# One evacuation per 16-row score, in a box of two PSUM banks, with all queues found anew

## Chip, cores and metric

The kernel runs on one core of a Trainium2 chip. The metric is device time in microseconds (us) of one execution, less is better. Engines are named as in the profile: PE (TensorE), DVE (VectorE), ACT (ScalarE), POOL (GpSimd), SP (SyncE, which issues the transfers).

## What is computed

A small neural codec: a depthwise filter of three taps over time, SiLU, four rounds of residual vector quantisation with codebooks of eight entries, and a second depthwise filter over the sum of the chosen entries.

```python
B, T, D, K = 2, 16000, 512, 3;  Nq, C = 4, 8          # all bf16
z = silu(sum(xp[:, i:i+T, :] * dw_enc[i] for i in range(K)))
res = z; q = 0
for s in range(Nq):
    cb = codebooks[s]
    d2 = |res|^2 - 2 res.cb^T + |cb|^2                # bf16 arithmetic, [B, T, C]
    sel = cb[d2.argmin(-1)]
    q = q + sel; res = res - sel
y = sum(qp[:, i:i+T, :] * dw_dec[i] for i in range(K))
```

## The kernel before, in words

**Tiles.** The 32,000 rows of time are cut into 18 tiles. A tile holds G rows of time on each of 128 partitions: G is 16 in fourteen of them, and 6 and 8 in the first and the last two. `split` (in the tile list) cuts a tile's G rows into stretches of SPLIT = 8 rows, so a 16-row tile has two.

**Stages of a tile.** Transposing loads bring x with its channels on the partitions (four groups of 128 channels). `front` works on one half (two channel groups) at a time: three taps as products with a weight per partition (lines 638 on ACT or 639 on DVE, into TA and TB), two additions of 4096 numbers (line 390, TA and ZB), the exponential on ACT (644), plus one (646 on DVE or 645 on ACT). `front2` does the reciprocal on ACT (656) and the product ZB <- ZB, EX (line 390), called the gate below. `select` scores the rows against the first three codebooks and decides one after the other (one-hot vectors OHA, OHD). `resid` subtracts the chosen entries from ZB on PE (833, 838) and casts the result back (860 on ACT or 861 on DVE), in four units of one channel group, each with a first and a second part, then scores the residual against the fourth codebook. `back` multiplies one-hot windows with the decoder's rows (910, 912, 914), casts the 1024 numbers to bf16 (919 on ACT or 920 on DVE, into YB) and stores them.

**A score.** `products` and `gram` let PE write 64 numbers for each row: 32 whose maximum is the row's squared norm (a mask product at line 668 sets the others very low), and the products with the 32 codebook entries (line 675). 8 rows fill one PSUM bank of 512 fp32. For each stretch of 8 rows `select` (key `score0`) evacuates with a reduce of 8 x 32 (line 709) and an addition of 8 x 24 (line 710), and `resid` (key `score3`) with a reduce of 8 x 32 (876) and a cast of 8 x 8 (877). All four run on DVE, and the bank comes free after them. Before the change a 16-row tile has two such boxes for each of its two scores.

**PSUM.** There are eight banks, as four pairs. `take=("S", box)` takes one bank, `take=("A", box)` an aligned pair. `resid` and `back` take pairs; `products` takes a pair when its stretch has more than 8 rows (`"SA"[g1 - g0 > NMK]`). At most four boxes may wait for DVE at a time.

**Order.** Nothing is scheduled at run time. Each step is put into a `Plan` with its engine, its readers and writers and a cost. Two long strings set the rest: RANK gives each step its place in its engine's queue, and WHERE says for each step that ACT or DVE could do (taps, plus one, casts out of PSUM) which of them does it. `Plan.order` walks the queues with the costs, hands out banks, and where it sees PE waiting for over a microsecond it puts fill matmuls in front of the next step (function `fill`, line 968: a product of 512 columns that nobody reads). Each engine then runs its queue in order and waits on semaphores.

Of the kernel before, what the change touches and what calls it, by code (L numbers as in the profile page):

```python
# [185 lines left out]
def kernel(  # L186
# [14 lines left out]
    KT = D // P  # L201
# [18 lines left out]
    RANK = ("0001020001010b0b0f0Z0g0W0i0Y0n04090n0o1c1q0n0x0q0y0h0l0r070R060k0D060A000s0j0l040E0e0C080f070v0a0g020c0e0h0i0j0l0o04050d"  # L220
            "0k0m0r0s0t02070g01030403080d0005060409060b050a0a0c0k0m0j0h0f090G0I0L0M0N0P0Q0l0q0s080t050J0j0o121718141e1s0q0f0i10151b0g"
            "080e090c0h0d030n0w0x0y070K0T0U0X0m0u0p0M0i0z03010t0B0a0m0o0H0r021f0v1k0b0u0F0p0e0V0k1a0c0O0d0S11130p16191d0w1g0A1p1i1j1h"
            "0z1l1n1m1o0B1v0C1y0D1A0r0s1I1J1K1M1N1O1P0p0t0J0u1R1T1U1W1X1Y1Z2021220q0v230w25262728292a2b2c0u0x0N0y0z2e0P0A0B2i2h0E0F0V"
            "0S0G0H0U0T0K0L2y2A2C2H2K0M2P0O120R130V0X351u1t1r1u1w1x0E1z1B0F0H1F1D1E1C1G0G1H1L0I0K0L2f0O2g0C0D2j2k2l2m2n2o2p0v0I2s0J2r"
            "2w2B2E2v2x2G2I2J2L0w0N0Z0P2N2Q2T2S2V2W2X2Y0x0Q110S0T15140U0V16190W0Y18370Z101b1a11123d3e3f3g3i131f1c1r171t1x1a1i161n1t03"
            "07020g080h0k060b0c0e0d0j09000f0a05241Q1S1V2d0R0Q2q0X2M2t2u2z0W2D0Y2F2R103317391c3h14153n18193t3u3v3x3z3B3D0y1b1l1d3G3I3L"
            "3M3K3N3O3P3Q3R0z1e1p1f3U3W3Y3X3Z4041420A1i441k1l1w1u1m1o1x1y1p1q1z1C1r1s1B4l1v1w4u1x1z4F4H4L4S4V1O1S20201W211V1V1V1X1Y1S"
            "1R1W23231Z212225242c0w0p0t0q0i0v0n0o0s0B0y0A0l0x0r0z0u0m2U302Z31323634381e1g3c1d3a3b3j3l3m3o1h3A1k3J1m3S1g1h431j1n494b4c"
            "4e4g4h4j0B1t4o1u4n4r4v4w4q4s4y4z4A4C0C1y4E1A4G4I4K4J4M4O4P4Q0D1C1G1E1F1J1I1H1J1N1M1K1L1P1O1M1N1Q1R1T1U5p1S1Z5z5E5H5J5M26"
            "5R2a272c292828262b28272r2l2x2r2n2s2m2t2p2t0T0N0F0D0S0K0E0R0M0P0Q0H0G0C0J0O0I0L3s3p3q3r3w1j3y3C1q451o3E3H3F3T1s3V461A4p1D"  # L230
            "4D1E4N1B1G4X1D1I4Z51525455572O580E1P1T1Q595b5e5g5l5n5o5q5t5v0G1Y5x225y5B5G5I5L5N5Q5S0I295W2e2g2c2b2h2i2e2d2k2m2k2g2n2o2j"
# [458 lines left out]
    def select(st):  # L690
        n, G = st["n"], st["G"]
        GC = G * C
        b = n % 2
# [119 lines left out]
    def resid(st):  # L813
        n, G = st["n"], st["G"]
        Z, W = zrows(st), OHR[n % 2]
# [48 lines left out]
        b = n % 2  # L864
# [141 lines left out]
```

## Time and profile before

| | us |
|---|---|
| median of three runs | 607.04 (604.66 to 607.81) |
| profiled execution, its time | 603.48 |
| its span, first to last instruction | 601.7 |
| PE busy, of it fill matmuls (L968) | 526.0, 131.9 |
| DVE busy | 567.5 |
| ACT busy | 547.5 |
| POOL busy | 60.7 |

Busy is the time in which at least one instruction of the engine was recorded. A matmul's record is longer than the time for which it holds up the next one, and the same holds for DVE and ACT instructions by a tenth of a microsecond. A group's row gives line, engine, operation, output <- inputs, shapes and count, then busy time and mean nanoseconds of one, then the engine's idle time just before the group and what ended it. A row of the timeline gives start and length in us. The granted TensorE clock was 0.994 over the span.

### The profile page before, as it was taken

The page shows a single profiled execution, that of the slowest core. Times are in us where ns is not written, and L with a number is a line of the kernel's source. Part 1 is how long each engine was busy: PE and PEld are TensorE (multiplying, and loading weights), DVE is VectorE, ACT ScalarE, POOL GpSimd, SP SyncE. Part 2 cuts the span into 40 slices and gives each one's busy share as a digit, 9 for nine tenths or more (in the row PEclk, how much of TensorE's full clock was granted, in tenths as well). Part 3 has the DMA queues.
Part 4 walks back from the last instruction along what each step waited for, and adds up shares of the span by engine and source line. Part 5 has one row for each costly group of instructions (what it writes and reads, how often), then busy time and mean ns, then how long its engine had stood idle before and what let it go on. Part 6 is the DMA issues. An engine that isn't in the chain of part 4 may idle for free.

```text
span 601.7 us, 28081 instructions
## 1 busy us (share of the span) xinstructions
PE 526.0 (87%) x12774; PEld 250.9 (42%) x12774; DVE 567.5 (94%) x1130; ACT 547.5 (91%) x423; POOL 60.7 (10%) x93
## 2 busy tenths in 40 slices
PE   5968889898888898899899888989988889989995
PEld 3424444334344344343444443443444344444552
DVE  6999999999999999999999989999999999999774
ACT  4898899999999999999999999999999999997554
POOL 3003100203101100000010011000001210110000
PEclk9999999999999999999999999999999999999998
DMA  9416356435556766565665668565494472204345
GB/s 216 94 44 91 65 93 111 104 66 82 146 94 140 130 165 116 148 139 89 169 108 98 154 112 175 108 144 140 89 198 125 108 142 82 107 5 142 109 141 189
DMA packets 155566, 71.87 MB, mean 119 GB/s; under 512 B 146895, under 2 KB 146927, under 8 KB 155318
## 3 DMA queue, kind: packets, MB, share of 16 engines
q1 hardware_dynamic: 155230, 69.64, 52.6%
q8 instruction: 100, 1.64, 1.1%
q10 hardware_dynamic: 216, 0.43, 0.4%
q14 instruction: 20, 0.16, 0.1%
HBM read 2.26 MB, written 32.77 MB: 58 GB/s over the span
## 4 chain that ended last, share of the span: by engine, by line
DVE 39%; ACT 19%; PE 17%; SPq 10%; issue 9%; DMA 4%; DVEq 0%; ACTq 0%
DVE ZB L390 8%; SPq L597 7%; DVE TB L639 6%; DVE TA L390 5%; PE banks L833 5%; ACT YB L919 5%; ACT EX L644 4%; DVE TA L639 4%; PE banks L838 3%; PE banks L910 3%; ACT EX L656 3%; PE banks L675 3%; ACT TB L638 2%; DVE EX L646 2%; ACT ZB L860 2%
## 5 line engine op out<-in xcount | busy, mean ns | idle before, releaser
L968 PE MATMUL banks<-MSK,IDENT 128*128 128x512 bf16 x555 | 131.9, 380 | 4.8 <-issue 2.3
L860 ACT CAST ZB<-banks 128x1024 bf16<-128x1024 f32 (+2 forms) x116 | 102.3, 938 | 20.1 <-PE banks L838 20.0
L644 ACT ACTIVATE EX<-ZB 128x4096 bf16<-128x4096 bf16 (+2 forms) x36 | 115.2, 3202 | 4.9 <-DVE ZB L390 4.7
L919 ACT CAST YB<-banks 128x1024 bf16<-128x1024 f32 x113 | 109.4, 1037 | 8.4 <-PE banks L910 7.1
L656 ACT ACTIVATE EX<-EX 128x4096 bf16<-128x4096 bf16 (+2 forms) x36 | 114.7, 3196 | 0.2
L675 PE MATMUL banks<-ZB 128*32 128x64 bf16 x8064 | 88.5, 196 | 5.1 <-DVE ZB L390 2.5
L675 PEld LDWEIGHTS <-ZB 128*32 128x32 bf16 x8064 | 75.4, 94 | 39.5 <-issue 33.6
L639 DVE TENSOR_SCALAR TB<-XT,WENC 128x2048 bf16<-128x2048 bf16 (+2 forms) x123 | 83.4, 689 | 0.8 <-DMA out_dram<-YB 0.5
L910 PE MATMUL banks<-WDEC,OHW 128*128 128x512 bf16 x252 | 73.2, 381 | 11.6 <-ACT ZB L860 3.2
L838 PE MATMUL banks<-OHR,WR 32*128 32x512 bf16 (+2 forms) x1152 | 82.0, 355 | 0.0
L747 POOL COPY OHD<-OHA 128x256 bf16<-128x256 bf16 (+2 forms) x36 | 39.6, 1099 | 401.6 <-DVE OHA L390 388.1
L968 PEld LDWEIGHTS <-IDENT 128*128 128x128 bf16 x555 | 50.6, 98 | 62.1 <-issue 8.0
L390 DVE TENSOR_TENSOR ZB<-TA,TB 128x4096 bf16<-128x4096 bf16 (+2 forms) x36 | 72.8, 2023 | 0.6 <-ACT TB L638 0.3
L390 DVE TENSOR_TENSOR TA<-TA,TB 128x4096 bf16<-128x4096 bf16 (+2 forms) x36 | 73.2, 2032 | 0.1
L390 DVE TENSOR_TENSOR ZB<-ZB,EX 128x4096 bf16<-128x4096 bf16 (+2 forms) x36 | 72.7, 2022 | 0.1
L833 PE MATMUL banks<-ZB,IDENT 64*64 64x512 bf16 (+2 forms) x576 | 55.5, 367 | 10.5 <-ACT ZB L860 3.8
L833 PE MATMUL banks<-ZB,UP 64*64 64x512 bf16 (+2 forms) x576 | 52.7, 351 | 0.0
L639 DVE TENSOR_SCALAR TA<-XT,WENC 128x2048 bf16<-128x2048 bf16 (+2 forms) x67 | 45.1, 681 | 3.0 <-DMA XT<-in_x_dram 2.0
L838 PEld LDWEIGHTS <-WR 32*128 32x128 bf16 x1152 | 23.3, 92 | 58.6 <-issue 50.4
L833 PE MATMUL banks<-ZB,DOWN 64*64 64x512 bf16 (+2 forms) x576 | 41.5, 363 | 0.0
L638 ACT ACTIVATE TB<-XT,WENC 128x2048 bf16<-128x2048 bf16 (+2 forms) x21 | 35.0, 1672 | 2.4 <-DVE TA L390 1.8
L646 DVE TENSOR_SCALAR EX<-EX 128x4096 bf16<-128x4096 bf16 (+2 forms) x33 | 36.8, 1115 | 0.0
(133 smaller groups left out, 591.3 us busy)
## 6 DMA issues: line engine op xcount, KB each, us to landing
out_dram<-YB SPq DMA_DIRECT2D x33, 448.0 KB
out_dram<-YB SPq DMA_DIRECT2D x28, 512.0 KB
XT<-in_x_dram SPq DMA_TRANSPOSE x267
out_dram<-YB SPq DMA_DIRECT2D x30, 60.0 KB
ZB<-in_x_dram SPq DMA_DIRECT2D x1, 1024.0 KB
ZB<-in_x_dram SPq DMA_DIRECT2D x1, 768.0 KB
out_dram<-YB SPq DMA_DIRECT2D x31, 2.0 KB
out_dram<-YB SPq DMA_DIRECT2D x2, 224.0 KB
```

Of the source, the lines that this page charges most:

```text
L390: add("DVE", cost, key, lambda: nc.vector.tensor_tensor(out=out, in0=a, in1=b, op=op), reads, writes, **kw)
L639: lambda dst=dst, src=src, w=w: nc.vector.tensor_scalar(out=dst, in0=src, scalar1=w, scalar2=None, op0=ALU.mult),
L644: add("ACT", act(2 * R), ("exp", n, h), lambda: nc.scalar.activation(v(ex), Z, ACT.Exp, scale=-1.0), zt, [("EX", sl), "ACTTAB"], hold="E")
L646: lambda: nc.vector.tensor_scalar(out=ex, in0=ex, scalar1=1.0, scalar2=None, op0=ALU.add), [], [("EX", sl)])
L656: nc.scalar.add_instruction(mybir.InstActivation(name=nc.get_next_instruction_name(), engine=mybir.EngineType.Activation, func=ACT.Reciprocal,
L675: nc.tensor.matmul(o[HB * q:HB * (q + 1), u * ZW:(u + 1) * ZW].rearrange("p (s c) -> p s c", s=2), lhsT=blk, rhs=both, start=False, stop=( ...
L833: nc.tensor.matmul(at(r)[to], lhsT=dia[h, h], rhs=Z[h, i, r:G:RG, :], start=start, stop=False)
L838: nc.tensor.matmul(at(r), lhsT=WR[v][g, i * P:(i + 1) * P], rhs=W[g, v // 3, 0:rows_of[r], :], start=False, stop=stop)
L860: either({"ACT": act_psum(2 * k * P), "DVE": dve(2 * k * P)}, key(1), lambda dst=dst, src=src: nc.scalar.copy(dst, src()), lambda dst=dst, ...
L910: nc.tensor.matmul(o, lhsT=W[:, k, PADC:PADC + P], rhs=WDEC[u], start=True, stop=not wrap)
L919: either({"ACT": act_psum(1024), "DVE": dve(1024)}, key, lambda dst=dst, box=box: nc.scalar.copy(dst, ps(box)), lambda dst=dst, box=box: n ...
L968: nc.tensor.matmul(PS[j // 2][:, 512 * (j % 2):512 * (j % 2) + NMK * ZW], lhsT=IDENT, rhs=MSK.rearrange("p u w -> p (u w)"), start=True, s ...
```

## The change

Both scores take all G rows of a tile as one stretch. For a 16-row tile the box is then a pair of banks; the two mask products, the 16 groups of row products and their order inside a score remain, and one reduce of 16 x 32 with one addition of 16 x 24 (or one cast of 16 x 8) follows the last of them. The first row products now wait for the ZB tokens of both stretches, which the gate and the casts write anyway. Tiles of 6 and 8 rows have one stretch as before.

With other steps in the plan, RANK and WHERE are replaced by new strings. They differ nearly everywhere, so the order of every queue and the engine of some taps, casts and additions are other ones, and so are the number and places of the fill matmuls, which follow from the order.

```diff
-    RANK = ("0001020001010b0b0f0Z0g0W0i0Y0n04090n0o1c1q0n0x0q0y0h0l0r070R060k0D060A000s0j0l040E0e0C080f070v0a0g020c0e0h0i0j0l0o04050d"
...
+    RANK = ("00010200010c0b0b0h0j0i0X0f0l0m02020j0q0w0A0n0v0p0x0j0p0u080H07030D0q0v040k0e0r020x0N0T090n070s0r0d0406090a0f0k0o0q010e0g"
...
-    WHERE = ("ADDDADDAAAADADDDDADDADDDDADDDADADADDAAAADAADDDDDADADDDDADADAAAAAAAADAAAAAAADDDDAADDDDAADDAADAAAAAAADAAAAAAAAADDDDDDADADDDD"
...
+    WHERE = ("AADAAAAAAAADDDDDDDDDDDDDDDDDADAAAADDAADAAADDDDDADADDDDADADAAAAAAADAAADAAADDDDADDDDDAADDADDAAAADADAADAAAAAADDDDDDDDDDDAD"
...
@@ select
-        zt = lambda q: [("Z", st["zb"], i, st["zq"] + q, b) for i in range(KT) for b in range(2)] + [("ZC", st["zb"])]
+        zt = lambda q: [("Z", st["zb"], i, st["zq"] + k, b) for k in range(len(st["split"])) for i in range(KT) for b in range(2)] + [("ZC", st["zb"])]
         nq = len(st["split"])
-        for q, (g0, g1) in enumerate(st["split"]):
+        for q, (g0, g1) in enumerate([(0, G)]):
@@ resid
-        zt = lambda q: [("Z", st["zb"], i, st["zq"] + q, b) for i in range(KT) for b in range(2)] + [("ZC", st["zb"])]
+        zt = lambda q: [("Z", st["zb"], i, st["zq"] + k, b) for k in range(len(st["split"])) for i in range(KT) for b in range(2)] + [("ZC", st["zb"])]
         nq = len(st["split"])
-        for q, (g0, g1) in enumerate(st["split"]):
+        for q, (g0, g1) in enumerate([(0, G)]):
```

91 lines of the change are left out of this document (45 added, 46 removed).

## Prediction, made before the changed kernel ran

> **What bounds the kernel now.** I read the page's busy lines first, then its slices, then busy time by window, then groups by form, and last the timeline around a score and at the end.
>
> ```profile
> span 601.7 us, 28081 instructions
> PE 526.0 (87%) x12774; PEld 250.9 (42%) x12774; DVE 567.5 (94%) x1130; ACT 547.5 (91%) x423; POOL 60.7 (10%) x93
> ...
> DVE  6999999999999999999999989999999999999774
> ACT  4898899999999999999999999999999999997554
> ```
> ```profile
> 0.00:60.00 60.00, 45.80 (x607) 23.95 (x611) 52.32 (x156) 44.59 (x60) 9.91 (x37) 1.00 0.56 111
> 60.00:540.00 480.00, 426.44 (x10656) 200.51 (x10656) 471.59 (x857) 468.48 (x325) 48.41 (x49) 1.00 0.56 118
> 540.00:555.00 15.00, 13.93 (x406) 6.24 (x403) 13.56 (x39) 11.31 (x11) 1.43 (x3) 1.00 0.41 143
> 555.00:592.00 37.00, 37.00 (x1105) 19.08 (x1103) 28.55 (x80) 20.12 (x27) 0.94 (x4) 1.00 0.38 131
> 592.00:602.00 10.00, 2.83 (x13) 1.09 (x12) 1.45 (x3) 3.03 (x4) 0.00 (x0) 0.82 0.57 177
> ```
> In a window row the columns are length, then busy time of PE, PEld, DVE, ACT and POOL. There are two regimes. From 60 to 540 us DVE is busy 471.59 of 480 us and ACT 468.48: DVE is idle for 8.4 us in all, ACT for 11.5. From 555 to 592 us PE is busy without a gap while DVE has 8 us and ACT 17 us to spare. The border is the last gate, the product that finishes the encoder output of the last tile:
>
> ```profile
> 548.05 0.41 PE L833 MATMUL banks<-ZB,IDENT 64*64 64x512 bf16 x4
> ...
> 550.25 0.41 PE L833 MATMUL banks<-ZB,IDENT 64*64 64x512 bf16 x4
> ...
> 552.91 0.95 DVE L390 TENSOR_TENSOR ZB<-ZB,EX 128x1536 bf16<-128x1536 bf16 x1
> ...
> 554.96 0.34 PE L668 MATMUL banks<-MSK,IDENT 128*128 128x384 bf16 x1
> ...
> 593.28 2.91 ACT L919 CAST YB<-banks 128x1024 bf16<-128x1024 f32 x3 [1.16 <-PE banks L910]
> ```
> It ends at 553.86; PE starts the last tile's first score at 554.96, and 46.7 us later the span ends. So I forecast in two pieces: how much DVE and ACT must do up to the last gate, and how much PE has behind it.
>
> **What one instruction costs its engine.** Recorded lengths overlap, so I take start to start:
>
> ```profile
> 304.91 0.42 DVE L876 TENSOR_REDUCE rr<-banks 128x8 bf16<-128x256 f32 x1
> 305.25 0.21 DVE L877 CAST PR<-banks 128x64 bf16<-128x64 f32 x1
> 305.38 0.28 DVE L725 TENSOR_TENSOR RC<-banks,S 128x128 f32<-128x128 f32 x1
> 305.58 0.28 DVE L390 TENSOR_TENSOR V<-PR,rr 128x128 bf16<-128x128 bf16 x1
> ...
> 537.78 3.80 ACT L919 CAST YB<-banks 128x1024 bf16<-128x1024 f32 x4
> 538.35 0.29 DVE L736 TENSOR_REDUCE M<-KEY 128x16 f32<-128x128 f32 x1
> 538.67 0.29 DVE L390 TENSOR_TENSOR OHA<-KEY,M 128x128 bf16<-128x128 f32 x1
> ...
> 540.00 0.35 DVE L710 TENSOR_TENSOR S<-banks,CC 128x192 f32<-128x192 f32 x1
> 540.26 0.17 DVE L390 TENSOR_TENSOR TR<-rr,RD 128x16 bf16<-128x16 f32 x1
> ```
> A reduce of 256 numbers holds DVE for 0.34 us, a cast of 64 for 0.13, an addition of 192 for 0.26, one of 128 for 0.20, each 0.08 less than its recorded length. From 64 to 256 numbers that is 0.21 us for 192, so about 1.05 ns a number over a fixed 0.065 us. An instruction that needs the one just before it starts 0.32 us after it (538.35 to 538.67) and not 0.20: 0.12 lost. On ACT four casts of 1.04 take 3.80, so 0.92 each.
>
> **The change, part by part.** (1) Evacuations. A 16-row score has one pair of DVE instructions over 16 rows instead of two pairs over 8:
>
> ```profile
> L709 DVE TENSOR_REDUCE rr<-banks 128x8 f32<-128x256 f32 x30 | 12.5, 417 | 0.6 <-PE banks L675 0.6
> L710 DVE TENSOR_TENSOR S<-banks,CC 128x192 f32<-128x192 f32 x30 | 10.4, 347 | 0.0
> L876 DVE TENSOR_REDUCE rr<-banks 128x8 bf16<-128x256 f32 x30 | 12.5, 417 | 1.8 <-PE banks L675 1.8
> L877 DVE CAST PR<-banks 128x64 bf16<-128x64 f32 x30 | 6.4, 213 | 0.0
> ...
> L920 DVE CAST YB<-banks 128x1024 bf16<-128x1024 f32 x13 | 15.9, 1219 | 4.7 <-PE banks L910 2.6 <-ACT ZB L860 1.0 <-PE banks L914 1.0
> L919 ACT CAST YB<-banks 128x1024 bf16<-128x1024 f32 x113 | 109.4, 1037 | 8.4 <-PE banks L910 7.1 <-ACT EX L644 0.7 <-DMA out_dram<-YB 0.3
> L861 DVE CAST ZB<-banks 128x1024 bf16<-128x1024 f32 x17 | 20.6, 1215 | 0.2 <-PE banks L838 0.2
> L860 ACT CAST ZB<-banks 128x1024 bf16<-128x1024 f32 x95 | 91.8, 1026 | 10.5 <-PE banks L838 10.4
> L639 DVE TENSOR_SCALAR TB<-XT,WENC 128x2048 bf16<-128x2048 bf16 x98 | 72.4, 750 | 0.6 <-DMA out_dram<-YB 0.5
> L638 ACT ACTIVATE TB<-XT,WENC 128x2048 bf16<-128x2048 bf16 x14 | 28.0, 2006 | 1.0 <-DVE TA L390 0.7
> L646 DVE TENSOR_SCALAR EX<-EX 128x4096 bf16<-128x4096 bf16 x27 | 33.2, 1230 | 0.0
> L645 ACT ACTIVATE EX<-EX 128x4096 bf16<-128x4096 bf16 x1 | 3.6, 3622 | 0.0
> ...
> L968 PE MATMUL banks<-MSK,IDENT 128*128 128x512 bf16 x555 | 131.9, 380 | 4.8 <-issue 2.3 <-DVE S L710 1.0 <-ACT ZB L860 0.9
> ```
> The number of elements stays, so each merged pair saves one fixed part: 14 tiles x 4 kinds = 56 instructions x 0.065 = 3.7 us of DVE (by differences of recorded length, 0.15 each, it would be 8.3, but the next instruction covers the rest). That two banks are read in one go should cost nothing: L920 reads two banks, and 1.219 less 0.08 is the 0.065 + 1024 x 1.05 ns of the same law. I keep 0 to 8.3 us as bounds.
>
> The Trainium skill, "Perfetto Trace Analysis", section "Optimizing Scalar/DVE Operations", puts DVE's fixed part at about 125 ns for PSUM. By it the saving would be an estimated 7 us and the forecast some 3 us lower; the starts above speak for half of it.
>
> (2) Latency. The evacuation can only begin when all 16 rows stand, and takes 0.60 + 0.47 us where the second half took 0.34 + 0.26: 0.47 us later for the decisions behind it, twice a tile. Up to 540 us DVE fills that with other tiles' work; without that cover 28 scores would cost 13 us. The score takes a pair of banks in place of one, twice; PE's 555 fill matmuls say that it has time to wait.
>
> (3) The new queues are the large part. I counted both built programs' queues by form and multiplied by start-to-start times. On DVE ahead of the last gate: evacuations -3.6; YB casts 4 to 19, +15 x 1.14 = +17.1; ZB casts +3.1 (three more of 1024); taps -2.8 (six fewer of 2048 at 0.67, some small ones more); the added ones (L646) -1.6; start-up copies -1.9; one-hot copies and the rest -0.9. Sum **+9.5 us**, from 517.2 to 526.7. On ACT up to the last reciprocal: YB -15 x 0.90 = -13.6, ZB -3.4, taps +8.3 (six more of 2048 at 1.9), L645 +4.9, start-up copies +2.8, rest +0.7: **-0.3**, of 514. Most of it stands by tile 9: at that tile's first gate DVE has 291.2 us behind it instead of 278.8, and the lead stays 6 to 13 us but for one gate. So ACT gets no relief and DVE gets more. DVE's work of 517.2 us took until 552.9, so 36 us went to waits, set-up and dependent pairs; pairs rise from 134 to 143, +1.1 us. What could pay back is DVE's idle time of 8.4 us between 60 and 540 us; it is scattered (2.4 us of it before L876 and L709). I take 2 us back, with 0 and 8.4 as bounds.
>
> (4) PE behind the last gate. In the built queue, behind the start of the last tile's first score, stand 1152 matmuls instead of 1115: the second part of one 16-row residual unit (16 of L833, 16 of L838; 548.05 to 550.25 shows 2.2 us from one second part to the next unit), seven small ones, 0.3, and two fills fewer, -0.4: **+2.1 us** in the stretch where PE has no gap. SP issues the same number of transfers, GpSimd the same copies.
>
> (5) Fill matmuls go from 555 to 698, in every part of the run: 143 x 0.22 (start to start) = 31 us of PE. PE has 75 us in which it isn't busy, so I cost them at nothing; where a fill stands while real work is ready, it costs 0.22 each.
>
> Sum: +9.5 + 1.1 - 2 + 2.1 = **+10.7 us**. The profiled execution took 603.48 us (span 601.7), so 614.2. The three timed runs lie at 604.66, 607.04 and 607.81, 1 to 4 us above it; around the middle of all four, 605.7, the sum gives **616 us**.
>
> **Rivals.** A. *DVE's idle time is paid back, and the tail packs tighter: faster.* Place: DVE's 8.4 us before 540 and the 6 us of the 46.7 in which PE's remaining 40 us of work don't run. It decides once more than 12.7 us (9.5 + 1.1 + 2.1) come back; all 14.4 and 2 more from start-up would give 603.5 - 4 = 599.5. Against it: fewer, longer evacuations remove at most 2.4 us of waits on PE, and nothing in the queues shortens the tail. Chance 0.12.
>
> B. *Half is paid back: no change.* The work is moved, yet waits shrink by 8 to 12 us, because ACT's 0.3 us and 15 fewer casts unlock it. 605 to 609 us. Chance 0.15.
>
> C. *PE becomes the bound.* If half the new fills stand in front of ready work, PE is up to 15 us later at the places where DVE and ACT wait for it (ACT waited 10.4 us before L860 already): 616 + 5 to 15, so 621 to 631. For it: PE is busy 426 of 480 us and 31 us of fills would make that nearly 455. Against it: no group waits long on PE now. The same would come of a pair of banks that isn't free for a score. Chance 0.13.
>
> D. *DVE's 9.5 us and PE's tail show in the span*: my forecast, 610 to 622. Chance 0.60.
>
> A rule speaks against the change in the tail: the Trainium skill, same page and section, says that where Vector isn't saturated but causes bubbles elsewhere, smaller instructions may finish sooner. In the tail DVE is not saturated; it would cost here an estimated 0.47 us for the one 16-row score that stands there.
>
> **How the numbers follow.** A measurement of this kernel can tell about 0.5%, 3 us, from no change: faster means below 604, slower above 610. A gives 0.12 of faster; B gives 0.13 of no change and 0.01 on either side of it; C and D give slower, with 0.03 of D's low end in no change. Faster 0.13, same 0.16, slower 0.71. Range: up to 625 takes in D and C's lower half; down to 603 takes in B. It leaves out most of A and C's upper end, under 2 in 10. D alone: 610 to 622.
>
> **What would show it.** In the new profile: L709 and L876 each x14 at about 0.68 us and L710 at 0.55 (fixed part right); DVE busy at or above 570 us and 26 L920 casts; the last gate (L390 ZB from EX, 1536 numbers) at about 562 us instead of 552.9; from there to the end about 49 us instead of 47.7, PE without a gap. A last gate at or before 554 would make my first piece wrong; a longer tail with idle PE, the second; waits of ACT on L838 above 30 us would speak for C.

## The result, and the profile after

| us | before | after |
|---|---|---|
| median of the runs | 606.75 (604.66 to 607.81, four) | 628.97 (624.79 to 632.84, four) |
| profiled execution | 603.48 | 626.47 |
| its span | 601.7 | 624.7 |
| last gate (start) | 552.9 | 571.3 |
| from there to the end | 48.8 | 53.4 |

The ratio is 1.037, with a 95% interval of 1.029 to 1.045: 22 us slower. I had said 616 and up to 625, so the sign was right and the size half of what came. In the changed kernel the lines are one lower than in the kernel before (its L709 is L708 here).

The head of the page of the changed kernel:

```profile
span 624.7 us, 28334 instructions
PE 552.6 (88%) x12917; PEld 262.9 (42%) x12917; DVE 575.1 (92%) x1075; ACT 553.3 (89%) x422; POOL 60.0 (10%) x93
...
DVE  6999999999999998999899989899999999998652
ACT  4797899999999999997898999899997999997564
```

DVE has 7.6 us more to do and ACT 5.8, over a span that is 23 us longer. Eights have come into the middle of DVE's row, and eights and sevens into ACT's, where there were nines. The same in busy time by window (length, then PE, PEld, DVE, ACT, POOL):

```profile
0.00:60.00 60.00, 44.66 (x599) 23.65 (x599) 52.20 (x157) 43.17 (x59) 5.73 (x35) 1.00 0.57 117
60.00:540.00 480.00, 435.89 (x10253) 204.62 (x10253) 465.42 (x770) 451.15 (x302) 50.76 (x49) 1.00 0.57 115
...
571.00:578.00 7.00, 7.00 (x188) 2.80 (x184) 5.54 (x16) 3.19 (x4) 0.29 (x1) 1.00 0.55 191
578.00:615.00 37.00, 34.64 (x988) 17.64 (x981) 22.77 (x65) 21.47 (x28) 1.00 (x4) 1.00 0.38 131
```

From 60 to 540 us DVE is now idle for 14.6 us (8.4 before) and ACT for 28.9 (11.5). In the stretch of 37 us near the end that had no gap on PE, PE is idle for 2.4 us. Groups by form:

```profile
L918 ACT CAST YB<-banks 128x1024 bf16<-128x1024 f32 x100 | 97.7, 1020 | 21.0 <-PE banks L909 18.5 <-PE banks L913 1.6 <-ACT YB L918 0.5
L859 ACT CAST ZB<-banks 128x1024 bf16<-128x1024 f32 x92 | 89.0, 1018 | 15.7 <-PE banks L837 15.6
L674 PE MATMUL banks<-ZB 128*32 128x64 bf16 x8064 | 88.6, 196 | 13.6 <-issue 9.9 <-DVE ZB L389 3.4
...
L919 DVE CAST YB<-banks 128x1024 bf16<-128x1024 f32 x26 | 31.6, 1217 | 5.3 <-PE banks L909 5.3
...
L875 DVE TENSOR_REDUCE rr<-banks 128x16 bf16<-128x512 f32 x14 | 9.6, 686 | 3.5 <-PE banks L674 1.7 <-ACT EX L655 1.7
L708 DVE TENSOR_REDUCE rr<-banks 128x16 f32<-128x512 f32 x14 | 9.6, 683 | 1.8 <-PE banks L674 1.8
L709 DVE TENSOR_TENSOR S<-banks,CC 128x384 f32<-128x384 f32 x14 | 7.6, 545 | 0.0
```

PE's row products in the kernel before:

```profile
L675 PE MATMUL banks<-ZB 128*32 128x64 bf16 x8064 | 88.5, 196 | 5.1 <-DVE ZB L390 2.5 <-issue 2.3 <-ACT ZB L860 0.2
```

The evacuations are as forecast: 14 of each kind, 0.69, 0.68 and 0.55 us. What is new is that ACT waits for PE: 18.5 us ahead of L918 (7.1 ahead of the same cast before), and PE's row products (L674) wait 13.6 us where they waited 5.1, most of it for "issue", which is nothing that another engine could release. Two gates show where the changed kernel falls behind; DVE's timeline of the changed kernel:

```profile
317.76 2.28 DVE L389 TENSOR_TENSOR ZB<-ZB,EX 128x4096 bf16<-128x4096 bf16 x1
```
```profile
571.29 0.96 DVE L389 TENSOR_TENSOR ZB<-ZB,EX 128x1536 bf16<-128x1536 bf16 x1 [0.44 <-ACT EX L655]
```

and that of the kernel before:

```profile
302.71 2.28 DVE L390 TENSOR_TENSOR ZB<-ZB,EX 128x4096 bf16<-128x4096 bf16 x1
```

From 52 to 214 us the gates of both kernels agree within 1.3 us. Tile 9's first gate (302.71 before, 317.76 after) is 15 us late, the one at 462 us is 20 us late, the last one 18. So the changed kernel falls behind between 214 and 462 us, and by another 4.6 us behind the last gate. A late gate is not all waiting: some 12 of the 15 us at tile 9's first gate are DVE work that the new queues put ahead of it, as the prediction had counted.

**An account of DVE up to the last gate.** I add the start-to-start time of every DVE instruction (that of its form where the next one follows at once), DVE's idle time, from its first instruction on, and what is left over, which is mostly dependent pairs. Before: 512.7 + 16.7 + 23.2. After: 521.9 + 23.7 + 24.7. So +9.2 of work, +7.0 of idle time, +1.5 of pairs; DVE's first instruction is also 0.5 us later. The account closes by construction: it says that DVE has 9 us more to do, not that these 9 us are why the gate is late.

### The profile page after: what moved, and what is told of

Its sections match the earlier page's. It is cut to its first block, busy times and chain, and to the rows that moved or that the text cites. A ratio compares the mean times of both kernels' runs of the same rounds, so it can differ in the third digit from the quotient of the medians.

```text
span 624.7 us, 28334 instructions
## 1 busy us (share of the span) xinstructions
PE 552.6 (88%) x12917; PEld 262.9 (42%) x12917; DVE 575.1 (92%) x1075; ACT 553.3 (89%) x422; POOL 60.0 (10%) x93
## 4 chain that ended last, share of the span: by engine, by line
DVE 41%; PE 25%; ACT 14%; SPq 9%; issue 8%; DMA 2%; DVEq 0%; ACTq 0%
DVE ZB L389 9%; SPq L596 8%; PE banks L832 5%; DVE TA L389 5%; DVE TB L638 5%; PE banks L674 5%; PE banks L837 4%; PE banks L909 4%; ACT EX L655 4%; DVE TA L638 3%; ACT EX L643 3%; PE banks L967 3%; ACT ZB L859 3%; DVE YB L919 3%; DVE EX L645 3%
## 5 line engine op out<-in xcount | busy, mean ns | idle before, releaser
L967 PE MATMUL banks<-MSK,IDENT 128*128 128x512 bf16 x698 | 165.6, 382 | 0.5 <-issue 0.5
L859 ACT CAST ZB<-banks 128x1024 bf16<-128x1024 f32 (+2 forms) x114 | 100.6, 930 | 27.5 <-PE banks L837 27.3
L918 ACT CAST YB<-banks 128x1024 bf16<-128x1024 f32 x100 | 97.7, 1020 | 21.0 <-PE banks L909 18.5
L674 PE MATMUL banks<-ZB 128*32 128x64 bf16 x8064 | 88.6, 196 | 13.6 <-issue 9.9
L674 PEld LDWEIGHTS <-ZB 128*32 128x32 bf16 x8064 | 74.7, 94 | 55.0 <-issue 49.9
L967 PEld LDWEIGHTS <-IDENT 128*128 128x128 bf16 x698 | 64.1, 98 | 73.3 <-issue 5.2
L638 DVE TENSOR_SCALAR TB<-XT,WENC 128x2048 bf16<-128x2048 bf16 (+2 forms) x119 | 80.1, 687 | 2.2 <-DMA XT<-in_x_dram 1.6
L746 POOL COPY OHD<-OHA 128x256 bf16<-128x256 bf16 (+2 forms) x36 | 35.7, 992 | 458.7 <-DVE OHA L389 438.9
L832 PE MATMUL banks<-ZB,IDENT 64*64 64x512 bf16 (+2 forms) x576 | 54.0, 365 | 9.9 <-ACT ZB L859 3.4
L637 ACT ACTIVATE TB<-XT,WENC 128x2048 bf16<-128x2048 bf16 (+2 forms) x25 | 45.6, 1822 | 2.5 <-DVE TA L389 2.0
L919 DVE CAST YB<-banks 128x1024 bf16<-128x1024 f32 x26 | 31.6, 1217 | 5.3 <-PE banks L909 5.3
```

Of the source, the lines that this page charges most:

```text
L638: lambda dst=dst, src=src, w=w: nc.vector.tensor_scalar(out=dst, in0=src, scalar1=w, scalar2=None, op0=ALU.mult),
L674: nc.tensor.matmul(o[HB * q:HB * (q + 1), u * ZW:(u + 1) * ZW].rearrange("p (s c) -> p s c", s=2), lhsT=blk, rhs=both, start=False, stop=( ...
L832: nc.tensor.matmul(at(r)[to], lhsT=dia[h, h], rhs=Z[h, i, r:G:RG, :], start=start, stop=False)
L859: either({"ACT": act_psum(2 * k * P), "DVE": dve(2 * k * P)}, key(1), lambda dst=dst, src=src: nc.scalar.copy(dst, src()), lambda dst=dst, ...
L918: either({"ACT": act_psum(1024), "DVE": dve(1024)}, key, lambda dst=dst, box=box: nc.scalar.copy(dst, ps(box)), lambda dst=dst, box=box: n ...
L919: lambda dst=dst, box=box: nc.vector.tensor_copy(dst, ps(box)), [], [("Y", y)], free=box, after=[j])
```

## Experiments

Eighteen kernels ran in seven groups. Each group had its own runs of the kernel before, and "over before" is the difference of medians to those. The letters of theories hold inside one expectation, and theories are named in words between them. "Border waits" are explained in the first part and count from 60 us on.

| kernel | median us | over before | ratio, 95% | border waits | last gate |
|---|---|---|---|---|---|
| before | 606.75 | | | 6.2 | 552.9 |
| changed | 628.97 | +22.2 | 1.029 to 1.045 | 21.9 | 571.3 |
| a_aligned | 622.98 | +17.7 | 1.024 to 1.033 | 21.3 | 570.5 |
| a_thin28 | 629.03 | +23.8 | 1.034 to 1.044 | 21.1 | 574.1 |
| b_drift | 612.60 | +7.3 | 1.009 to 1.019 | 23.2 | 559.4 |
| a_shift | 623.95 | +19.8 | 1.023 to 1.037 | 15.4 | 571.9 |
| b_shift | 621.10 | +17.0 | 1.018 to 1.034 | 32.5 | 561.5 |
| a_thin_all | 633.53 | +30.4 | 1.047 to 1.053 | 29.4 | 578.9 |
| a_thinwin | 628.93 | +25.8 | 1.036 to 1.047 | 24.7 | 573.6 |
| a_halves | 630.22 | +25.0 | 1.036 to 1.047 | 21.4 | 575.4 |
| a_split | 624.76 | +21.7 | 1.033 to 1.039 | 12.2 | 572.8 |
| b_heavy | 613.91 | +7.8 | 1.004 to 1.020 | 7.5 | 562.9 |
| a_light | 627.71 | +21.6 | 1.028 to 1.042 | 23.4 | 574.4 |
| a_lightwin | 627.84 | +24.7 | 1.034 to 1.047 | 33.0 | 573.8 |
| a_lightnof | 620.11 | +17.0 | 1.019 to 1.036 | 15.8 | 568.1 |
| s_full | 622.85 | +20.4 | 1.029 to 1.038 | 15.0 | 570.8 |
| s_part | 610.88 | +8.4 | 1.010 to 1.019 | 10.5 | 561.2 |
| b_late | 621.27 | +16.6 | 1.023 to 1.031 | 13.0 | 570.8 |
| b_blocks | 677.79 | +73.1 | 1.117 to 1.123 | 19.2 | 625.5 |
| b_merged | 681.47 | +75.3 | 1.117 to 1.131 | 16.4 | 623.4 |

The granted TensorE clock differs from run to run, and within one kernel the time goes with it: the changed kernel took 626.5 and 624.8 us at a clock of 0.996 and 0.991, and 631.5 and 632.8 at 0.982 and 0.979. Over the runs of the kernels in the table, without a_thin_all, 0.01 less of clock goes with some 3 us more; that is an estimate from these runs. Where two kernels differ in clock, a part of their difference goes with that.

### PE's instruction groups

The new waits of PE have no engine behind them. PE's timeline of the changed kernel, around the longest but one:

```profile
303.72 0.39 PE L667 MATMUL banks<-MSK,IDENT 128*128 128x512 bf16 x1
304.04 0.62 PE L674 MATMUL banks<-ZB 128*32 128x64 bf16 x56
307.59 0.24 PE L674 MATMUL banks<-ZB 128*32 128x64 bf16 x8 [2.92 <-issue]
307.76 1.25 PE L967 MATMUL banks<-MSK,IDENT 128*128 128x512 bf16 x5
```

A run of 64 products that needs 0.69 us undisturbed is cut after 56 of them, for 2.92 us. Counting PE's weight loads through the trace, waits of over 0.3 us of this kind stand at one place in every 128: load 97 in the kernel before, load 96 in the changed one. The transfers of the instruction queue (q8) are packets of 16,384 bytes, 101 of them for 12,917 matmul-and-load pairs; that makes 256 instructions, or 128 pairs, to a packet. In 16 of the 18 waits of the changed kernel a packet began 2.2 to 2.9 us before PE went on (for this wait at 305.37). So PE's program comes in groups of 128 pairs, and where PE runs through one group faster than the next comes in, it waits at the border. Where the changed kernel waited, the group had taken 2.2 to 5.8 us with the wait. 128 matmuls of 64 columns take 1.3 us, so a merged score with its 258 matmuls crosses two borders in quick succession.

The Trainium skill, "Runtime: NRT & Kernel Launch", section "Instruction fetch mechanics", gives the same block of 256 instructions and calls the cost of crossing a border mostly hidden. The size agrees with the trace. The cost doesn't here: 21.9 us in the changed kernel and 6.2 in the one before.

The kernel's plan knows of this (it counts matmuls in chunks of 128), but `products` counts one mask product per score while `gram` issues one per 8 rows. With merged scores 28 matmuls go uncounted, and every border drifts away from where the plan put it.

**a_aligned**: 28 of the 698 fills are left out, each the nearest to a 16-row score, so that the borders fall again where the plan has them.

```diff
+    for i in need:                       # the 28 second halves
+        j = min((j for j in left if left[j] > 0), key=lambda j: abs(at[j] - at[i]))
+        left[j] -= 1
+        steps[j]["cut"] += 1
...
-                fill(*s["fill"])
+                j, k = s["fill"]
+                fill(j, k - s["cut"])
```

> The changed kernel with 28 of its 698 fill matmuls left out, one for each 16-row score, each out of the block nearest to that score. The plan counts one mask product for a 16-row score and PE runs two, so the groups of 256 instructions in which PE's program arrives end up to 28 matmuls earlier than the plan thinks; leaving 28 out puts them back. Theory F (PE waits for its instructions): PE's idle time that ends without a visible cause falls from 16 us before the last gate to under 9, and the time by 3 to 8 us from 626 to 633. Theory L (fill matmuls stand in front of ready work): 28 x 0.22 = 6 us less of PE, so at most 6 us as well, but the waits at the group borders stay and the control with thin fills shows the same. Theory Q (the 23 us are DVE's longer queue alone): no change.

**a_thin28**: its control. The same 28 fills stay, 64 columns wide.

```diff
+                thin(j, s["cut"])
```

> Control: the changed kernel with the same 28 fill matmuls kept, but 64 columns wide in place of 512, so that PE's stream keeps its length and its group borders. Theory F: PE's idle time without a visible cause stays near 16 us and the time within 2 us of the changed kernel's. Theory L: the same gain as from leaving them out, up to 6 us.

**b_drift**: the kernel before with the drift alone, one uncounted matmul of 64 columns per 16-row score.

```diff
+            if u == 0 and g0 > 0:
+                nc.tensor.matmul(ps(box)[:, 0:ZW], lhsT=IDENT, rhs=MSK[:, 0, :], start=True, stop=True)
```

> The kernel before with one added matmul of 64 columns in each 16-row score, 28 in all, of which the plan knows nothing; queues, fills and evacuations are as before. The added work is some 28 x 0.03 = 1 us of PE. Theory F: PE's waits at the group borders go from 4.6 us to 15 to 20 and the time rises by 5 to 10 us. Theories L and Q: at most 1 us more.

Aligning gave 6.0 us (622.98 against 629.03 for its control, in one group; the two intervals don't touch), though the same PE time was cut in the control but for 28 x some 0.06 us. By the estimate above, some 2 of the 6 us go with the granted clock (0.981 to 0.996 in a_aligned, 0.982 to 0.987 in the control). The drift alone cost the kernel before 7.3 us, at DVE work that was the same within 0.1 us up to the last gate and at nearly the same clock (0.980 to 0.990 against 0.986 to 0.995). The expectation of a_aligned had the waits fall to under 9 us. Their sum hasn't fallen; they have moved, most of them to places ahead of fills:

```profile
PE banks L967 <- issue: 17.6, 36, 2.9
...
PE banks L674 <- issue: 7.6, 17, 1.5
```

These rows are PE's waits in a_aligned (total, times, longest). 17.6 us stand ahead of fills (L967; 0.5 in the changed kernel), and the row products have 7.6 us in place of 9.9, none longer than 1.5. Some matmul records are missing in this trace; by the weight loads, whose records are complete, the border waits ahead of row products fell from 11.2 to 5.7 us. So what border waits cost here was set by their place and not by their sum.

**a_shift** and **b_shift**: the first block of fills is replaced by more and narrower ones, so that all later borders move, by 112 matmuls in the changed kernel and by 48 in the one before.

```diff
+    more = 112                           # b_shift: 48
...
-            if s["fill"]:
+            if s["fill"] and more and s["fill"][1] >= 20:
+                narrow(s["fill"][0], s["fill"][1] + more)      # 32 columns
+                more = 0
+            elif s["fill"]:
```

> The changed kernel, all queues, fills, boxes and evacuations as they are, but its first block of 54 fill matmuls of 512 columns (in set-up, at about 30 us) is replaced by 166 of 32 columns. That shifts every later border between groups of 256 PE instructions by 112 matmuls, to places where, by the plan's own order, PE seldom crosses two borders in quick succession. Theory F: PE waits at borders in front of real work fall from 20 us to under 8, and the time falls by 4 to 8 us from 629, to 621 to 625. If F is wrong: no change beyond 1 us.

> The kernel before with the same edit, but 48 matmuls more (102 of 32 columns for 54 of 512), which puts the borders where dense stretches of PE cross them. Nothing else differs. Theory F: waits at borders rise from 6 to 25 us or more and the time by 8 to 16 us, to 612 to 620. If F is wrong: no change beyond 1 us.

The changed kernel won 2 to 5 us (by +19.8 in place of +22.2, or by the medians), and the intervals overlap. The kernel before lost 17.0, with no other change of work, and its border waits rose to 32.5 us. That the old queues depend on where their borders fall agrees with b_drift, but the 17 us aren't clean. The narrow fills at the start also lower the granted clock there:

```profile
PEclk9788989998999999999999999999999999999999
```

That is b_shift, in slices of 15 us. Its profiled execution was its fastest (614.6); there it is 5.9 us late at 149 us already, behind the slices below 9, and 8.6 us at the last gate. How much of the 5.9 is the clock isn't settled. Its four runs go with their clock, too: 614.6 and 618.7 us at 0.973 and 0.975, 623.5 and 623.8 at 0.964.

### The fills

**a_thin_all**: all 698 fills have 64 columns in place of 512. **a_thinwin**: only the 164 that the plan puts between 180 and 325 us.

```diff
-                fill(*s["fill"])
+                thin(*s["fill"])                                       # a_thin_all
+                fill(*s["fill"], 64 if 180 < s["t"] < 325 else 512)    # a_thinwin
```

> The changed kernel with all 698 fill matmuls 64 columns wide in place of 512; same queues, same number of PE instructions, same group borders. It takes 698 x 0.19 = 130 us of work off PE. Theory L (fill matmuls stand in front of ready work): 5 to 15 us faster than 629, if the granted clock holds. Theory N: within 3 us of 629, or slower where the PE clock falls because PE does less.

> The changed kernel, where the 164 fill matmuls that the plan puts between 180 and 325 us have 64 columns instead of 512 (some 0.16 us less each, 26 us of PE in all; the number of instructions and so the borders of PE's instruction groups stay). Theory D (DVE's work alone sets the end of that stretch): no change, 627 to 631 us at a kernel before of 606, tile 9's first gate within 2 us of 317.8. Theory C (PE, held by fills, sets it): tile 9's first gate at or below 312 and 5 us or more off the whole. Theory B (PE is held by its instruction groups, and shorter fills only move the wait to the border): no gain, and at least 5 us more of waits at borders.

Two lines of the page of a_thin_all:

```profile
PE 465.7 (74%) x12917; PEld 242.7 (38%) x12917; DVE 576.0 (91%) x1075; ACT 552.8 (87%) x422; POOL 60.3 (10%) x93
...
PEclk9757777596977989889899987989987999999998
```

PE was busy for 87 us less and the kernel took longer (+30.4 over before in place of +22.2): the granted clock fell to 0.884 (0.996 with long fills), and the border waits rose to 29.4 us. In a_thinwin, with 18 us less of PE, the time is that of the changed kernel (628.93) and tile 9's first gate is at 321.9. The third possibility in a_thinwin's expectation, 5 us more of border waits, came halfway (24.7 against 21.9). But the granted clock fell in the very stretch where the fills were cut. From 215 to 320 us, the changed kernel and then a_thinwin (the clock is the third number from the end):

```profile
215.00:320.00 105.00, 94.77 (x2338) 44.17 (x2334) 100.01 (x166) 95.06 (x65) 6.24 (x9) 0.98 0.62 123
```
```profile
215.00:320.00 105.00, 80.32 (x2284) 39.49 (x2280) 96.01 (x156) 91.52 (x62) 4.69 (x9) 0.89 0.70 124
```

So taking the fills away buys nothing, because the real matmuls then run at a lower clock. Whether the fills stand in the way at full clock is not shown by these two kernels. The chain of waits that ended last says that some do: up to the last gate fills make 2.2 us of it in the kernel before and 19.0 in the changed one. As far as the profile's semaphores tell, a fill on the chain means that the step behind it was released before the fill ended.

### The merged box and its one evacuation

**a_halves**: the changed kernel, where each 16-row score is still one box in the same queues, but is read by two pairs of DVE instructions over 8 rows.

```diff
-                nc.vector.tensor_reduce(out=rr[0][:, g0:g1, 0], in_=v[:, :, 0:HB], axis=AX.X, op=ALU.max)
+                for h0 in range(g0, g1, SPLIT):
+                    h = slice(h0, min(h0 + SPLIT, g1))
+                    nc.vector.tensor_reduce(out=rr[0][:, h, 0], in_=v[:, h, 0:HB], axis=AX.X, op=ALU.max)
...
```

> The changed kernel with each 16-row evacuation issued as two pairs of 8 rows again, out of the same pair of banks, all at its place; every queue, bank and PE's stream are unchanged. 56 more DVE instructions at 0.065 us are 3.7 us. If DVE sets the pace the time rises by 2 to 4 us; if PE's lateness leaves DVE room, by under 1.5 us.

**a_split**: the new queues on the old steps. Two boxes of one bank and two pairs per score, with the first pair directly ahead of the second, and a plan that counts both mask products.

```diff
-    RANK = ("0001020001010b0b0f0Z0g0W0i0Y0n04090n0o1c1q0n0x0q0y0h0l0r070R060k0D060A000s0j0l040E0e0C080f070v0a0g020c0e0h0i0j0l0o04050d"
+    RANK = (the changed kernel's, with each first evacuation put back ahead of the second)
...
```

In this diff and the last one below the ranks are given in words.

> The change undone inside the new queues: each 16-row score has two boxes of one bank again, each evacuated by its own pair of instructions, the first pair put directly ahead of the second; all other steps keep the new order and the new choice of engine. The plan now counts every mask product. Theory M (the merged box itself costs time: a free pair of banks comes late and PE and DVE wait for all 16 rows): 610 or less. Theory N (the new order and engine choice are what costs, whatever the box): the time stays above 620; against the changed kernel it loses the 3.7 us that merging saves DVE and gains the 6 us of the realigned instruction groups, so 623 to 630.

Splitting the evacuation adds 3.8 us of DVE work (578.9 against 575.1), what was forecast, and 1 to 3 us of time, which the intervals can't tell from none. a_split has no merged box at all and is 21.7 us over before. So the box of two banks and the long evacuation, which are what the change is named after, are worth next to nothing either way once the new strings are given. What costs is in the strings. a_split doesn't part their order from their choice of engine: up to its last gate DVE has 13 us more work than in the kernel before (9.2 by the strings, 3.8 by the evacuations) and 5.4 us more idle time.

### DVE's work

**b_heavy** puts the work on the kernel before, **a_light** takes it out of the changed one.

```diff
-                nc.vector.tensor_reduce(out=rr[0][:, g0:g1, 0], in_=v[:, :, 0:HB], axis=AX.X, op=ALU.max)
+                for _ in range(2 if G == 16 and g0 == 0 else 1):
+                    nc.vector.tensor_reduce(out=rr[0][:, g0:g1, 0], in_=v[:, :, 0:HB], axis=AX.X, op=ALU.max)
...
```

> The kernel before, with the first reduce of each 16-row score issued twice in a row (28 more reduces of 256 numbers on DVE, each 0.34 us start to start: 9.5 us of DVE work, nothing else moved; the output is the same). Theory D (DVE's work ahead of the last gate shows one for one in the time): 8 to 11 us over the kernel before, the last gate at 561 to 564 us instead of 552.9, DVE's idle time as before. Theory X (something else bounds, and DVE's 16.7 us of idle time take the work up): less than 4 us over the kernel before, and the idle time falls by 6 us or more.

```diff
+    LIGHT = [(2, 1), (3, 3), (4, 0), (4, 1), (4, 3), (5, 0), (5, 1), (5, 5), (6, 3)]
...
-                       lambda dst=dst, box=box: nc.vector.tensor_copy(dst, ps(box)), [], [("Y", y)], free=box, after=[j])
+                       lambda dst=dst, box=box, c=64 if (n, k) in LIGHT else 1024: nc.vector.tensor_copy(dst[:, 0:c], ps(box)[:, 0:c]), [], [("Y", y)], free=box, after=[j])
```

> The changed kernel, where nine of the YB casts on DVE, all between 185 and 325 us, copy only 64 of their 1024 numbers (so part of the output is left out): 9 x 1.0 = 9 us of DVE work less, as much as the change put on DVE ahead of the last gate. Theory D: 7 to 10 us less than the changed kernel, so 619 to 622 us at a kernel before of 605, and tile 9's first gate at about 309 us instead of 317.8. Theory X: no more than 3 us less, and DVE's idle time 6 us or more above the changed kernel's.

In the kernel before the work shows: the last gate is 10.0 us later for 9.3 us of work, and the time 7.8 us longer (interval 2.5 to 12), just under the 8 of theory D. In the changed kernel it doesn't: with DVE's work back at the kernel before's (within half a microsecond up to the last gate), the time is 627.71, +21.6 over before in place of +22.2, and DVE's idle time is 17.3 us above the kernel before's. The 9.2 us of my account were there, and taking as much away where the loss arises gave nothing. Pieces of the chain of waits of a_light (start, length, what) show what takes over:

```profile
229.32 1.67 PE banks L968 x7
231.21 1.30 PE banks L674 x128
232.51 0.22 PE banks L784 x2
232.73 2.06 issue
234.79 0.51 PE banks L784 x6
235.56 4.01 PE banks L968 x10
239.57 0.99 PE banks L832 x16
```

The chain stays on PE here, through products, a border wait and fills (32.8 us of fills up to the last gate). That suggested a test with the fills taken out as well:

**a_lightwin** is a_light with a_thinwin's short fills, **a_lightnof** is a_light with those 164 fills left out.

```diff
-            if s["fill"]:
+            if s["fill"] and not 180 < s["t"] < 325:     # a_lightnof
```

> The kernel with nine DVE casts cut to 64 numbers (part of the output left out; it took as long as the changed kernel, with DVE idle for 9 us more and a chain of waits that runs through PE between 227 and 322 us) and with the same 164 fills at 64 columns. Theory CD (DVE's work and PE's fills each hold that stretch when the other is taken away): tile 9's first gate at or below 312 us instead of 319.1, and 5 us or more off the whole, 616 to 623 us. Theory B: no gain, since PE crosses its groups no faster, and the waits at borders grow by 5 us or more.

> As the last, with those 164 fills left out instead of made short (the nine casts cut as well): 1.3 groups of instructions less, and all later borders move by 36 matmuls. Theory CD: as the last or some 2 us faster. Theory B: up to 1.3 x 4 = 5 us faster than with short fills, since fewer instructions have to come in.

Neither brought tile 9's first gate to 312 us (316.8 and 319.8), so theory CD fell as it was stated. But the clock from 215 to 320 us was 0.93 and 0.90 in these two (0.98 in a_light), so they don't show either what the fills hold at full clock. What holds PE in that stretch, fills, borders or the place of its work, stays open. a_lightnof took 7.7 us less than a_lightwin, but behind the stretch: at 382 us the gates of both are 13 us later than in the kernel before, at the last gate 21 us in a_lightwin and 15 in a_lightnof. Behind 325 us the two have the same queues, fills and evacuations; what differs is where the borders fall (the border waits fell from 33.0 to 15.8 us) and the clock (0.97 and 1.00 from 325 to 570 us).

### The order of a merged score

**s_full**: the changed steps with a plan that counts both mask products, and queues improved from the new ones by many small moves. **s_part**: only 17 of the 28 scores merged, in queues reached from the old ones by small moves.

```diff
-                    mm=(r1 - r0) * 16 + (r0 == g0))
+                    mm=(r1 - r0) * 16 + ((r0 - g0) % NMK == 0))
...
-        for q, (g0, g1) in enumerate(st["split"]):
+        for q, (g0, g1) in enumerate([(0, G)] if (n, 0) in ONE else st["split"]):     # s_part
```

> The whole change (all 28 scores of 16 rows in one box, one evacuation each) with queues improved once more: starting from the new strings, the plan now counts both mask products, and small moves of steps within a queue and between ACT and DVE were kept where the plan's own walk became shorter; by it the order gained 8 us. If the order and not the merged box carries the loss (theory N), 611 to 619: 6 us less for the counted products and up to 8 for the order. If the merged box itself carries it (theory M): 620 or more.

> 17 of the 28 scores merged, in queues that started from those of the kernel before and were then improved by the same small moves. 34 DVE instructions fewer, 2.2 us at 0.065. Theory N: with the old order nearly kept the time is 600 to 608, no slower than before beyond 0.5%. Theory M: the loss grows with the number of merged scores, 17/28 of some 17 us, so 612 to 616.

By its time s_full came out as theory M had it, s_part between the two theories. By the counts of its forms s_full has some 3 us less DVE work up to the last gate than the changed kernel, and s_part no more than the kernel before; their DVE idle time is 10.6 and 6.5 us above the kernel before's. The loss is +8.4 with 17 merged scores and +20.4 with all 28, in queues that differ as well. The miscount doesn't explain it, since both plans count both mask products. That better queues for merged scores could be found is not ruled out.

The last three kernels take a merged score apart in the old queues. **b_late** moves only each first evacuation in DVE's queue, to directly ahead of the second. **b_blocks** also moves the first half's row products in PE's queue, to directly ahead of the second half's. **b_merged** then has one box and one evacuation. The number of fills follows from the plan's walk: 555 in the kernel before, 552, 773 and 737 in these three.

```diff
     RANK: old strings, and for every 16-row score
+    rank[evac 1] = rank[evac 2] - 0.5                                     # b_late, b_blocks
+    rank[products 1] = rank[products 2] - 0.5                             # b_blocks, b_merged
-        for q, (g0, g1) in enumerate(st["split"]):                        # b_merged
+        for q, (g0, g1) in enumerate([(0, G)]):
```

> The kernel before with two one-bank boxes and two pairs of DVE instructions per 16-row score as ever, but with each first pair moved down DVE's queue, to directly ahead of the second (some 5 us later); PE's queue as before. It has the late first evacuation of a merged score and nothing else of it. Theory L (the late evacuation, which holds a bank and puts both pairs behind all 16 rows, is what a merged score costs): 40 us or more over the kernel before. Theory P (PE's block of all 16 rows costs): less than 25 us over it.

> As the last, with the first half's row products moved down PE's queue as well, to directly ahead of the second half's, so that PE issues 258 matmuls in one block, still into two boxes of one bank with two pairs of DVE instructions. It has the order of the merged scores in the old queues and not their merged box and instructions. Theory P: close to the merged kernel in the old queues, 60 to 80 us over the kernel before. Theory L: about as the last kernel. A box of two banks that has to be waited for, or the one long evacuation (theory E): 20 us or more less than the merged one's +75.

> The kernel before with all 28 16-row scores in one box and one evacuation, but with the old queues: the first half's products stand directly ahead of the second's, the first evacuation is dropped, the plan counts both mask products. Theory M (a merged score takes away freedom of order: DVE gets its decisions later and PE has to issue 258 matmuls in one block, and new queues have to buy that back): more than 20 us over the kernel before, so over 625 us, with DVE's work 3 to 4 us less than before and its idle time at least 20 us more. Theory Q (the merge costs nothing, and only the new queues lost the time): at or below the kernel before, 600 to 608 us.

The late evacuation costs 16.6 us, so theory P held. PE's block of all 16 rows, with the 218 more fills that the plan puts around it, costs another 56, and the merged box with its single evacuation 2 more, within the intervals nothing, although it saves DVE 3.4 us up to the last gate. DVE's work is the kernel before's within 0.1 us in the first two; nearly all that they lose is idle time (+14.0 and +67.9 us). DVE's evacuations by form, first in b_late, then in b_blocks:

```profile
L709 DVE TENSOR_REDUCE rr<-banks 128x8 f32<-128x256 f32 x30 | 12.5, 416 | 2.6 <-PE banks L675 2.6
L876 DVE TENSOR_REDUCE rr<-banks 128x8 bf16<-128x256 f32 x30 | 12.5, 415 | 3.2 <-PE banks L675 3.0
```
```profile
L709 DVE TENSOR_REDUCE rr<-banks 128x8 f32<-128x256 f32 x30 | 12.6, 419 | 26.9 <-PE banks L675 26.8
L876 DVE TENSOR_REDUCE rr<-banks 128x8 bf16<-128x256 f32 x30 | 12.5, 417 | 17.8 <-PE banks L675 17.8
```

The same instructions at the same lengths wait 44.6 us for PE's row products in place of 5.6. The chain that ended last has moved to PE; its shares of the span in the kernel before, the changed one, and b_blocks:

```profile
DVE 39%; ACT 19%; PE 17%; SPq 10%; issue 9%; DMA 4%; DVEq 0%; ACTq 0%
```
```profile
DVE 41%; PE 25%; ACT 14%; SPq 9%; issue 8%; DMA 2%; DVEq 0%; ACTq 0%
```
```profile
PE 37%; DVE 29%; ACT 20%; issue 9%; DMA 2%; SPq 1%; ACTq 0%; DVEq 0%
```

Of b_blocks' share fills make 59 us up to the last gate (12 in b_late). So its 56 us are the price of the block together with the fills that come with it. No run parts the two. Two rows of DVE's timeline of the kernel before show what was given up:

```profile
296.70 0.42 DVE L876 TENSOR_REDUCE rr<-banks 128x8 bf16<-128x256 f32 x1
304.91 0.42 DVE L876 TENSOR_REDUCE rr<-banks 128x8 bf16<-128x256 f32 x1
```

These are the two halves of one score, 8.2 us apart. Over the 28 scores of 16 rows the second reduce starts 1.2 to 17.6 us behind the first, 5.4 on the mean. In that time all engines do other tiles' work. A merged score takes these two places away and leaves one.

## Why the prediction was right, and where it failed

**What held.** The law for one DVE instruction: reduces of 512 numbers took 0.68 and 0.69 us, the addition of 384 took 0.55, and splitting them again cost 3.8 us for a forecast of 3.7. The count of DVE's work ahead of the last gate: +9.2 us measured, +9.5 forecast. Dependent pairs and the like: +1.5 against +1.1. PE's work in the tail, by the windows from the last gate to the end, before and after:

```profile
553.00:602.00 49.00, 41.84 (x1149) 20.91 (x1145) 32.00 (x83) 23.32 (x30) 0.94 (x4) 0.96 0.40 135
```
```profile
571.00:625.00 54.00, 44.71 (x1180) 21.52 (x1172) 28.80 (x81) 28.80 (x36) 1.29 (x5) 0.98 0.44 147
```

PE is busy for 2.9 us more; +2.1 was forecast. That fills cost nothing, (5), is neither shown nor refuted: shorter fills gained nothing, but at a lower clock, and fills stand on the chain of waits for 19.0 us where they stood for 2.2.

**Where it failed first: the reading of the count.** "ACT gets no relief and DVE gets more" made DVE's 9.5 us the main term. It would have been right in the old order (b_heavy: 7.8 us of time for 9.3 of work). In the changed kernel, taking 9 us away between 185 and 325 us gained nothing (a_light). I had taken the bound of the kernel before for that of the changed one.

**The step that failed: the latency, (2).** I priced a merged score by the length of its DVE instructions, "0.47 us later for the decisions behind it, twice a tile", and let other tiles' work hide it, so it stands in the sum at nothing. But the first halves were evacuated 5.4 us ahead of the second ones on the mean, and the merge moves the first half's products and evacuation by that. Moving the first evacuation alone costs 16.6 us in the old queues (b_late), at DVE work that is the same, with 14.0 us more of DVE idle time: the cover that I counted on did not hold. A part of the 16.6 may be borders, whose waits are 13.0 us there in place of 6.2. With PE's block and its fills it is 75 us. The new queues win back about 53 of these; no queues tried here won the rest. That the order costs is shown in the old queues. That it is also what remains in the new ones is argued from a_aligned and s_full, which still lose 17.7 and 20.4 us without the miscount.

**The idle time.** "I take 2 us back, with 0 and 8.4 as bounds": DVE's idle time up to the last gate rose by 7.0 us. Both bounds were on the side of a gain, and nothing in the working allowed for a loss. In the sum this term is 9.0 us of the 12 that are missing between the forecast +10.7 and the +23.0 of the two profiled executions; the tail is another 2.5. I read this idle time as the latency of (2); in the changed kernel no run shows that.

**The tail.** From the start of the last gate to the end it is 4.6 us longer and not 2.1 (48.8 to 53.4; the "47.7" of the prediction ran from the gate's end). Besides PE's 2.9 us, its idle time went from 7.2 to 9.3 us in the two windows above; border waits make 1.9 us of that.

**The rivals.** C named PE, and its 621 to 631 us hold the result. Its mechanism, fills ahead of ready work, was not settled here: the chain of waits speaks for it and the tests with shorter fills ran at a lower clock. Its sign was "waits of ACT on L838 above 30 us":

```profile
ACT ZB L859 <- PE banks L837: 27.3, 29, 2.8
ACT YB L918 <- PE banks L909: 18.5, 15, 2.6
```

These waits of the changed kernel stood at 20.0 and 7.1 us before. The sign just missed the bound on the first line, and the casts of YB, which I hadn't named, had the rest. PE does hold ACT here; what holds PE is in part its program's borders (a_aligned, b_drift). I had PE's wait for "issue" ahead of L968 in a quoted row and took no price from it.

**The size, put together.** Undoing the drift of 28 uncounted matmuls gave 6 us (a_aligned against a_thin28; some 2 of them go with the clock), and the drift alone cost 7 (b_drift). The prediction had no term for it. That isn't a fixed price: three kernels without the miscount are 17.7 (a_aligned), 20.4 (s_full) and 21.7 us (a_split) over before. What remains of the 22 us I put down to the order of merged scores; in the changed kernel that is argued and not shown. Open stays how PE's 56 us in the old order divide between the block, its fills and the borders: the border waits of b_blocks are 6 us above b_late's, its fills on the chain 47 us. No kernel here beats the kernel before.

## What to carry to other kernels

Before two evacuations are merged, look up in the timeline how far apart they stand, because the merge moves the first producer and the first consumer by that, and the saved fixed cost of an instruction (here 0.13 us a pair) is small beside it. A closed account of the busiest engine isn't yet a cause: take the work away and see whether the time follows, and look at the granted clock of the stretch before reading the result. Where many short matmuls run in a row, count them against the blocks in which the program comes in, and keep any model of these blocks in step with what is issued.

## What I had not expected of the hardware

- PE's program comes in packets of 16,384 bytes, and a group of 128 matmul-and-load pairs that PE passed in 2.2 to 5.8 us ended in waits of up to 3.2 us in the changed kernel. Moving the borders by 28 matmuls changed the time by 6 us (a_aligned, some 2 of them with the clock) and 7 us (b_drift), and perhaps by more in b_shift.
- Fill matmuls that nobody reads hold the granted clock: 0.996 with 698 of 512 columns, 0.884 with the same number of 64. With 164 of them shortened in one stretch the clock fell in that stretch from 0.98 to 0.89 (a_thinwin, 215 to 320 us). Fills that seem idle may thus pay for the speed of the matmuls around them.
